# DeltaNet with Fourier mixing: an inversion given to 4 steps a slot instead of 6, its end and load 12's products placed in the mixing, one state copy on ScalarE

## The chip, the cores and the metric

One core of a Trainium2 chip runs the whole kernel in one launch. The metric is the device time of the core in microseconds. The engines are TensorE (PE, with its weight loads as PEld), VectorE (DVE), ScalarE (ACT), GpSimd (POOL) and SyncE (SP), whose queue issues most DMAs.

## The reference

The first half is a delta-rule recurrence over 4 batches x 8 heads, 768 tokens, head width 48; the second half takes its output as 4 x 768 x 384, adds the real part of a 2-D Fourier transform, normalizes, and applies a two-layer network of width 1536. All is float32.

```python
k_n = k / (norm(k) + 1e-6)
for t in range(768):                       # per batch and head, state is 48 x 48
    y[t] = q[t] @ state
    state += beta[t] * outer(k_n[t], v[t] - k_n[t] @ state)
x = y as (batch, token, head*48)
u = x + real(fft(fft(x, axis=token), axis=feature))
un = (u - mean(u)) / sqrt(var(u) + 1e-6)
out = u + relu(un @ w_ch1) @ w_ch2
```

## The kernel before

**Tiling.** The 768 tokens of a batch are cut into 6 loads of 128 (`NL` = 6), so there are 24 loads, `g` = 0 to 23, each of all 8 heads. A load has two chunks of 64 tokens. The recurrence inside a chunk is turned into products with the inverse of a triangular matrix; the state `S` goes from chunk to chunk.

**Inversions.** The triangular matrices of 4 loads (`RL` = 4) are inverted together on VectorE, in round `r`. Rounds 0 to 2 use `invert16`, rounds 3 to 5 `invert` (line 399). The fourth inversion is round 3, for loads 12 to 15. `invert` is a Python generator that yields 77 times: 14 steps of preparation (a transpose at L405, a square root on ScalarE at L412, small operations up to L440), then 31 pairs of a product into `tmp` (L446) and an addition to `M` (L450), and last both transposes (L453 into `A`, L454 into `G`). It has to be complete before `pre_m` of the first load of its round.

**Products of a load.** `pre_m` (line 558) makes for a load the matrices that the recurrence needs: GpSimd writes `MT` (L566) and scales `V` (L569), 16 products of `G` with `GX` go to PSUM (`px`), ScalarE copies them to `XM` (L582, a tile of tag "Q" that has one buffer), 16 more products with `A` (`py`), and ScalarE copies them to `MT` (L593). It yields after `XM` and at its end. Loads before 12 use `pre_m16` instead (Z, ND and MT at L608 to L651).

**The recurrence.** `step(g, c)` for batches after the first has three parts, one to each advance: A, products of `S` with `KT` and their subtraction from `V` on VectorE (L701); B, products of `V` with `MT`, copied to `U` by ScalarE (L711); C, products of `U` with `K`, added to the state `S` by VectorE (L742), or, for the first chunk of a batch, copied (L740). `outputs` makes the rows `x` (L765 on ScalarE, L775 on VectorE).

**Order.** `period(g, side)` runs one load in 6 slots (`SLOTS`). Slots 0 to 2 hold A, B, C of the first chunk and 3 to 5 those of the second; for the first load of a batch slot 0 is empty. In each slot come first these parts and pieces of the next loads' preparation, then some steps of the inversion under way (`advance(inv, n)`), then pieces of the folds, and last `side`, the network's products (`ph`, `po`) of the batch before, which fill TensorE. Round r+1 is begun in slot 1 of the second load of round r (load 9 for the fourth inversion). The order of instructions on each engine is the order of these calls. Loads 6 and 7 are an exception: there only TensorE has its order by hand, and the other engines are ordered by the framework's scheduler.

**Folds and mixing.** After the loads of a batch, `folds` (L798 to L816) adds and subtracts halves of `x` for the transforms; `fourier` is advanced 10 times: 4 parts with the transform over the tokens (`evt`, `odt`), and 6 with the transform over the features (`dtab`), each with a ScalarE copy to the tile `Q` (L876, the same single buffer as `XM`), four VectorE operations on `x` (L885 to L888) and the statistics (L892, L893; `rstd` on GpSimd). Between the parts come 12 pieces of `side`.

The lines that place the inversion and load 12's `pre_m` before the change:

```python
pieces[3 if fresh else 1].append(pm)          # fresh: g is the last load of a round
pieces[5 if fresh else 3].append(pm)
...
if i == (2 if r + 1 < R16 else 3) and fresh and inv:
    drain(inv)
...
elif inv:
    advance(inv, 8 if r + 1 < R16 else 6)
```

Load 11 is both the last load of round 2 and the last of batch 1.

Of the kernel before, what the change touches and what calls it, by code (L numbers as in the profile page):

```python
# [15 lines left out]
ACT = mybir.ActivationFunctionType  # L16
# [4 lines left out]
RL = 4  # L21
RING = 7
V16 = 16
R16 = 3
# [40 lines left out]
def kernel(  # L65
# [10 lines left out]
    nc = tc.nc  # L76
# [3 lines left out]
    NL = S // L  # L80
# [19 lines left out]
    def ps_pair():  # L100
        return ps.tile([128, 2, 512], F32, tag="pair", bufs=2, name="pair")

    def ps_one():
        return ps.tile([128, 512], F32, tag="one", bufs=2, name="one")
# [4 lines left out]
    def mm(o, lhsT, rhs, start, stop=True):  # L109
        nc.tensor.matmul(o, lhsT=lhsT, rhs=rhs, start=start, stop=stop, skip_group_check=True)  # L110
# [570 lines left out]
    def step(g, c):  # L681

        b, n = divmod(g, NL)
        begin = n == 0 and c == 0
        s0 = S.get((b, 2 * n + c))
        if b > 0:

            if c == 0:
                Us[g] = wk.tile([128, 2, 4, D], F32, tag="U0", bufs=2, name="U")
            K, MT, V = pre[g]  # L690
            U0, KT = Us[g], KTs[g]
            R, U = V[:, c], U0[:, c]
            if not begin:
                pw = ps_pair()
                for jj in range(2):
                    for hh in range(2):
                        for jp in range(2):
                            mm(pw[full[hh], jp, D * jj:D * jj + D],
                               KT[lo[jp], hh, jj, c * C:c * C + C], s0[lo[jp], hh, jj, :], jj == 0)
                R4 = R.rearrange("p (jj jp) e -> p jp jj e", jp=2)  # L700
                nc.vector.tensor_tensor(  # L701
                    R4, R4, pw[:, :, 0:2 * D].rearrange("p a (j e) -> p a j e", e=D),
                    op=ALU.subtract)
                yield
            pu = ps_one()
            for j in range(4):
                for hh in range(2):
                    mm(pu[full[hh], D * j:D * j + D],
                       MT[full[hh], 4 * c + j].rearrange("p b t -> p (b t)"), R[full[hh], j, :],
                       j == 0)  # L710
            nc.scalar.activation(U.rearrange("p j e -> p (j e)"), pu[:, 0:4 * D], ACT.Copy)  # L711
            yield
        else:
            K, WT = pre[g]
            U = Us[g][:, c]
        if not begin and b == 0:
            pw = ps_pair()
            for jj in range(2):
                for hh in range(2):
                    for jp in range(2):  # L720
                        mm(pw[full[hh], jp, D * jj:D * jj + D], WT[lo[jp], hh, c, jj, :],
                           s0[lo[jp], hh, jj, :], jj == 0)
            nc.vector.tensor_tensor(
                U.rearrange("p (jj jp) e -> p jp jj e", jp=2),
                U.rearrange("p (jj jp) e -> p jp jj e", jp=2),
                pw[:, :, 0:2 * D].rearrange("p a (j e) -> p a j e", e=D), op=ALU.subtract)
            yield
        if not (n == NL - 1 and c == 1):
            s1 = wk.tile([128, 2, 2, D], F32, tag="S", bufs=4, name="S")
            S[(b, 2 * n + c + 1)] = s1  # L730
            pk = ps_pair()
            for jj in range(2):
                for jp in range(2):
                    for hh in range(2):
                        mm(pk[full[jp], hh, D * jj:D * jj + D], K[full[hh], 4 * c + 2 * jj + jp, :],
                           U[full[hh], 2 * jj + jp, :], jj == 0)
            pk = pk[:, :, 0:2 * D]
            s1v = s1.rearrange("p h j e -> p h (j e)")
            if begin:
                nc.vector.tensor_copy(s1v, pk)  # L740
            else:
                nc.vector.tensor_tensor(s1v, s0.rearrange("p h j e -> p h (j e)"), pk,  # L742
                                        op=ALU.add)
            yield
# [226 lines left out]
    def advance(gen, n=1):  # L971
        for _ in range(n):
            if next(gen, "end") == "end":
                return False
        return True

    def drain(gen):
        for _ in gen:
            pass
# [31 lines left out]
    pm = inv = late = None  # L1011

    def period(g, side):


        nonlocal pm, inv, late, done, fold
        b, n = divmod(g, NL)
        r, li = divmod(g, RL)
        more = g + 1 < NLT
        last_round = (r + 1) * RL >= NLT  # L1020
        load_k(g + 2)
        c0, c1 = step(g, 0), step(g, 1)
        if n > 0:
            pieces = [[c0], [c0], [c0], [c1], [c1], [c1]]
        else:
            pieces = [[], [c0], [c0], [c1], [c1], [c1]]
        behind = [[] for _ in range(SLOTS)]
        if late:

            for i in (1, 2) if n == 1 and b == 1 else (0,):  # L1030
                pieces[i].append(late)
        if n + 1 < NL:
            late = outputs(g)
            if g > NL:
                pieces[4].append(late)
        else:

            pieces[5] = []
        fresh = more and li == RL - 1
        if more:  # L1040
            nq = pre_q(g + 1)
            behind[0].append(nq)
            pieces[2].append(nq)
            if g + 1 >= RL * R16:
                pm = pre_m(g + 1)
                pieces[3 if fresh else 1].append(pm)
                pieces[5 if fresh else 3].append(pm)
            elif g + 1 >= 2 * RL:
                pm = pre_m16(g + 1)
                if not fresh:  # L1050
                    behind[0].append(pm)
                for i in range(4):
                    pieces[i + (2 if fresh else 1)].append(pm)
        if not last_round and r > 1:
            if li == 0:
                load_beta(r + 1)
            keys = {0: ((0, 1), (2, 3), (4, 5)), 1: ((0, 1),)}.get(li, ())
            for i, (s0, s1) in enumerate(keys):
                k4 = pre_a(RL * (r + 1) + 3 * li + i)
                behind[s0].append(k4)  # L1060
                pieces[s1].append(k4)
        for i in range(SLOTS):
            if i == (2 if r + 1 < R16 else 3) and fresh and inv:
                drain(inv)
                inv = None
            for p in pieces[i]:
                advance(p)
            if i == 5 and n + 1 == NL:
                o = outputs(g)
                drain(o)  # L1070
                late = None
            if li == 1 and i == 1 and r > 1 and not last_round:
                inv = invert(r + 1)
            if g == NL:
                advance(inv, 5)
                advance(conv, 2 if i < 5 else 4)
            elif inv:
                advance(inv, 8 if r + 1 < R16 else 6)
            if n + 2 >= NL and 0 < i < 5:

                if n + 2 == NL and i == 1:
                    fold = folds(b)
                advance(fold, 2)
            at = SLOTS * n + i + 1
            if b > 1:
                want = 2 + (PIECES - KEEP - 2) * at // (SLOTS * NL)
            else:

                want = 2 + KF + (2 + 2 * KF) * at // (2 * SLOTS)
                if n > 1:  # L1090
                    want = 4 + 3 * KF + (PIECES - KEEP - 4 - 3 * KF) * (at - 2 * SLOTS) // (
                        SLOTS * (NL - 2))
            for p in behind[i]:
                advance(p)
            advance(side, want - done)
            done = max(want, done)
        load_v(g + 2)
# [3 lines left out]
    with tc.manual_schedule(engines=engines):  # L1101
# [212 lines left out]
        inv = invert16(2)  # L1314
# [5 lines left out]
    with tc.manual_schedule(engines=engines):  # L1320
        for b in range(1, B):
            for g in range(max(NL * b, NL + 2), NL * (b + 1)):
                period(g, side)

            advance(side, KEEP - 12)
            drain(fold)
            f, then = fourier(b), mlp(b)
            done = 0
            for i in range(4 + NC):
                advance(f)  # L1330
                advance(side, 12 * (i + 1) // (4 + NC) - done)
                done = 12 * (i + 1) // (4 + NC)
                if i in (6, 8):
                    advance(then)
            drain(side)
            side, done = then, 2
        drain(side)
# [30 lines left out]
```

## Time and profile before

| | us |
|---|---|
| median of 3 runs (742.43 to 745.95) | 743.56 |
| the profiled execution | 744.35 |
| its span, first to last instruction | 742.6 |
| TensorE busy in it | 689.8 |
| VectorE busy in it | 377.5 |
| ScalarE busy in it | 262.7 |
| GpSimd busy in it | 79.5 |
| mean granted clock of TensorE | 0.975 |

The profiled execution's own time is 0.79 us over the median and 1.75 us over its span. In the profile a row of the timeline has start, length, engine, line, operation, output and inputs, and in brackets the idle time before it and what ended it. L110 is the line of the helper for all matrix products and L113 of that for transposes on TensorE, so these are told apart by their tiles. Times are counted from the span's start: load 9 begins near 234 us, load 10 at 252.8, load 11 at 275.4, the mixing of batch 1 at 302.2, and load 12 at 332.7.

### The profile page before, as it was taken

The page shows a single profiled execution, that of the slowest core. Times are in us where ns is not written, and L with a number is a line of the kernel's source. Part 1 is how long each engine was busy: PE and PEld are TensorE (multiplying, and loading weights), DVE is VectorE, ACT ScalarE, POOL GpSimd, SP SyncE. Part 2 cuts the span into 40 slices and gives each one's busy share as a digit, 9 for nine tenths or more (in the row PEclk, how much of TensorE's full clock was granted, in tenths as well). Part 3 has the DMA queues.
Part 4 walks back from the last instruction along what each step waited for, and adds up shares of the span by engine and source line. Part 5 has one row for each costly group of instructions (what it writes and reads, how often), then busy time and mean ns, then how long its engine had stood idle before and what let it go on. Part 6 is the DMA issues. An engine that isn't in the chain of part 4 may idle for free.

```text
span 742.6 us, 23085 instructions
## 1 busy us (share of the span) xinstructions
PE 689.8 (93%) x10176; PEld 529.9 (71%) x10176; DVE 377.5 (51%) x957; ACT 262.7 (35%) x641; POOL 79.5 (11%) x138
## 2 busy tenths in 40 slices
PE   6877989977999978999999999999999999999998
PEld 4576878756767656878768778777677688777684
DVE  5877887699622996170596228288211241600000
ACT  5544763796324212224323343133223121211120
POOL 8000001120000101021100220030112100200000
PEclk9799989999999997999999999999999999999999
DMA  9842452153123211003212211001110000000000
GB/s 153 221 73 43 118 120 86 24 146 95 25 59 75 46 34 28 1 11 72 40 40 49 45 40 28 11 23 36 42 34 13 12 12 3 20 1 21 11 11 21
DMA packets 108791, 36.10 MB, mean 49 GB/s; under 512 B 101873, under 2 KB 105234, under 8 KB 108690
## 3 DMA queue, kind: packets, MB, share of 16 engines
q1 hardware_dynamic: 106866, 33.86, 21.0%
q8 instruction: 80, 1.31, 0.7%
q0 software_dynamic: 640, 0.43, 0.4%
q10 hardware_dynamic: 1184, 0.33, 0.3%
q14 instruction: 21, 0.17, 0.1%
HBM read 29.88 MB, written 4.72 MB: 47 GB/s over the span
## 4 chain that ended last, share of the span: by engine, by line
PE 73%; DVE 17%; ACT 6%; issue 2%; DMA 1%; DVEq 0%; ACTq 0%
PE po L110 24%; PE ph L110 21%; PE one L110 15%; PE pair L110 9%; PE one L113 2%; DVE M L450 1%; DVE tmp L446 1%; PE ptr L113 1%; PE unread L1114 1%; DVE M L520 1%; DVE tmp L517 1%; ACT GU L395 1%; DMA C<-in_k_dram 1%; DVE w L292 1%; ACT G L385 1%
## 5 line engine op out<-in xcount | busy, mean ns | idle before, releaser
L110 PE MATMUL po<-w,hT 128*128 128x384 f32 x576 | 204.8, 495 | 0.0
L110 PE MATMUL ph<-unT,w 128*128 128x256 f32 x828 | 197.9, 391 | 0.0
L110 PEld LDWEIGHTS ph<-unT,w 128*128 128x128 f32 x828 | 155.6, 193 | 23.3
L110 PEld LDWEIGHTS po<-w,hT 128*128 128x128 f32 x576 | 103.5, 190 | 56.5
L939 ACT ACTIVATE hT<-ph 128x256 f32<-128x256 f32 x138 | 52.9, 383 | 145.9 <-PE ph L110 145.0
L954 DVE TENSOR_TENSOR x<-x,po 128x384 f32<-128x384 f32 x24 | 13.2, 551 | 107.0 <-PE po L110 107.0
L742 DVE TENSOR_TENSOR S<-S,pair 128x192 f32<-128x192 f32 x40 | 14.0, 350 | 71.2 <-PE pair L110 71.1
L110 PEld LDWEIGHTS one<-V,MT 64*64 64x64 f32 x768 | 31.4, 144 | 18.6 <-issue 7.3
L885 DVE TENSOR_TENSOR x<-x,one 128x193 f32<-128x193 f32 x24 | 8.5, 355 | 67.7 <-ACT Q L876 67.7
L110 PE MATMUL one<-V,MT 64*64 64x48 f32 x768 | 36.8, 231 | 3.0 <-DVE V L701 2.7
L450 DVE TENSOR_TENSOR M<-M,tmp 128x31 f32<-128x31 f32 (+15 forms) x93 | 34.5, 371 | 3.2
L446 DVE TENSOR_TENSOR tmp<-A,M 128x31 f32<-128x31 f32 (+15 forms) x93 | 34.1, 367 | 2.5
L701 DVE TENSOR_TENSOR V<-V,pair 128x192 f32<-128x192 f32 x33 | 11.5, 349 | 38.2 <-PE pair L110 28.9
L110 PE MATMUL one<-MT,ND 64*64 64x64 f32 x768 | 29.4, 228 | 1.1 <-ACT MT L649 0.7
L897 POOL TENSOR_SCALAR rstd<-mv 128x1 f32<-128x1 f32 x24 | 6.9, 287 | 218.5 <-DVE mv L893 218.5
L110 PEld LDWEIGHTS one<-dtab,F 97*128 97x128 f32 (+1 forms) x192 | 25.1, 191 | 6.9 <-ACT KT L320 1.8
L320 ACT ACTIVATE QT<-one 128x512 f32<-128x512 f32 x24 | 14.3, 595 | 42.1 <-PE one L113 42.0
L110 PEld LDWEIGHTS one<-MT,ND 64*64 64x64 f32 x768 | 26.9, 143 | 2.5 <-ACT MT L624 1.1
L110 PEld LDWEIGHTS pair<-S,KT 48*64 48x64 f32 x528 | 10.8, 133 | 23.1 <-issue 10.4
L110 PE MATMUL one<-dtab,F 97*128 97x97 f32 (+1 forms) x192 | 26.0, 275 | 1.4 <-ACT KT L320 1.4
L566 POOL TENSOR_TENSOR MT<-A,pack 128x512 f32<-128x512 f32 x12 | 12.8, 1067 | 130.5 <-PE one L110 64.8
L110 PEld LDWEIGHTS pair<-U,K 64*64 64x64 f32 x704 | 15.0, 133 | 15.7 <-issue 12.2
(181 smaller groups left out, 1026.7 us busy)
## 6 DMA issues: line engine op xcount, KB each, us to landing
w<-in_moe_w_ch_dram SPq DMA_DIRECT2D x12, 384.0 KB, 7.4
E<-in_moe_w_ch_dram SPq DMA_DIRECT2D x12, 384.0 KB, 3.0
out_dram<-x SPq DMA_DIRECT2D x24, 192.0 KB, 1.9
K<-in_k_dram SPq DMA_DIRECT2D x92, 48.0 KB, 2.7
V<-in_v_dram SPq DMA_DIRECT2D x92, 48.0 KB, 2.2
C<-in_k_dram SPq DMA_DIRECT2D x18, 192.0 KB, 9.8
Q<-in_q_dram SPq DMA_DIRECT2D x18, 192.0 KB, 3.3
w<-in_q_dram SPq DMA_DIRECT2D x6, 192.0 KB, 7.6
```

The lines of the kernel that those rows point to most:

```text
L110: nc.tensor.matmul(o, lhsT=lhsT, rhs=rhs, start=start, stop=stop, skip_group_check=True)
L113: nc.tensor.matmul(o, lhsT=src, rhs=ident[0:src.shape[0], 0:src.shape[0]], is_transpose=True, start=start, stop=True, skip_group_check=True)
L292: nc.vector.tensor_tensor(pieces[i - lag][1].rearrange("p c f -> p (c f)"), man0, num0.bitcast(F32), op=ALU.mult)
L320: nc.scalar.activation(dst.rearrange("p h j t -> p (h j t)"), pt, ACT.Copy)
L446: nc.vector.tensor_tensor(t, A[:, j + 1:W, j:j + 1].broadcast_to([128, n, j + 1]), M[:, j:j + 1, 0:j + 1].broadcast_to([128, n, j + 1]), o ...
L450: nc.vector.tensor_tensor(M[:, j + 1:W, 0:j + 1], M[:, j + 1:W, 0:j + 1], t, op=ALU.add)
L566: nc.gpsimd.tensor_tensor(MT, MTd[:, m8, None, :].broadcast_to([128, 8, 2, W]), m_blk[:, None, :, None].broadcast_to([128, 8, 2, W]), op=A ...
L701: nc.vector.tensor_tensor(R4, R4, pw[:, :, 0:2 * D].rearrange("p a (j e) -> p a j e", e=D), op=ALU.subtract)
L742: nc.vector.tensor_tensor(s1v, s0.rearrange("p h j e -> p h (j e)"), pk, op=ALU.add)
L885: nc.vector.tensor_tensor(near, near, pb[:, 0, 0:MH + 1], op=ALU.add)
L939: nc.scalar.activation(hT[:, fc, :], ph, ACT.Relu)
L954: nc.vector.tensor_tensor(x[:, T, :], x[:, T, :], po, op=ALU.add)
```

## The change

`lone` is true for load 11 alone. The fourth inversion (`r + 1 == R16`) is advanced by 4 steps in each slot instead of 6. In load 11 it is not drained, and load 12's `pre_m` is not put into slots 3 and 5. In the loop over the mixing's 10 parts the inversion is advanced by 3 steps in each of parts 0 to 2 and drained in part 3; then `pre_m` of load 12 is advanced once in each part until it is over (parts 4 and 5). The condition on `NL * (b + 1) % RL` holds for batch 1 only among those with an inversion under way. Apart from that the first state of batch 1 (load 6, first chunk) is copied out of PSUM by ScalarE instead of VectorE. Loads, weights and all other calls stay.

```diff
-            if begin:
+            if begin and b == 1:
+                nc.scalar.activation(s1v, pk, ACT.Copy)
+            elif begin:
                 nc.vector.tensor_copy(s1v, pk)
...
         fresh = more and li == RL - 1
+
+        lone = fresh and n + 1 == NL
...
                 pm = pre_m(g + 1)
-                pieces[3 if fresh else 1].append(pm)
-                pieces[5 if fresh else 3].append(pm)
+                if not lone:
+                    pieces[3 if fresh else 1].append(pm)
+                    pieces[5 if fresh else 3].append(pm)
...
-            if i == (2 if r + 1 < R16 else 3) and fresh and inv:
+            if i == (2 if r + 1 < R16 else 3) and fresh and inv and not lone:
                 drain(inv)
                 inv = None
...
             elif inv:
-                advance(inv, 8 if r + 1 < R16 else 6)
+                advance(inv, 8 if r + 1 < R16 else 4 if r + 1 == R16 else 6)
...
             for i in range(4 + NC):
                 advance(f)
                 advance(side, 12 * (i + 1) // (4 + NC) - done)
                 done = 12 * (i + 1) // (4 + NC)
+                if inv and NL * (b + 1) % RL == 0:
+                    if i < 3:
+                        advance(inv, 3)
+                    elif i == 3:
+                        drain(inv)
+                    elif not advance(pm):
+                        inv = None
                 if i in (6, 8):
                     advance(then)
```

## The prediction

> **What bounds the kernel now.** I read the engine totals and the chain of waits first. TensorE is busy for 93% of the span and carries 73% of the chain; VectorE carries 17%, though it is busy only half of the time. So most stages run at TensorE's pace, and only the stages in which VectorE is in the chain can give anything.
>
> ```profile
> PE 689.8 (93%) x10176; PEld 529.9 (71%) x10176; DVE 377.5 (51%) x957; ACT 262.7 (35%) x641; POOL 79.5 (11%) x138
> PE 73%; DVE 17%; ACT 6%; issue 2%; DMA 1%; DVEq 0%; ACTq 0%
> ```
>
> The chain in order of time shows where: from 254.4 to 286.0 us it is almost only VectorE, and most of it L446, L450, L453 and L454, which are `invert(3)`. Its last lines (start, length, what):
>
> ```profile
> 278.36 1.00 DVE M L450
> 279.38 0.96 DVE tmp L446
> ...
> 282.20 1.97 DVE A L453
> 284.17 1.83 DVE G L454
> 286.00 0.23 DVE S L742
> ...
> 286.27 0.52 PE pair L110 x16
> ```
>
> From 286.27 to 332 it is TensorE alone. I then asked for the busy time of each engine in the stretch of the inversion and in the one behind it, up to the start of load 12 (two rows), and in slices of 4 us at the inversion's end:
>
> ```profile
> 243.90:287.80 43.90, 35.30 (x687) 25.98 (x686) 41.64 (x102) 8.69 (x20) 6.92 (x7) 0.95 0.18 39
> 287.80:332.70 44.90, 44.32 (x304) 34.69 (x305) 18.23 (x54) 11.88 (x33) 4.18 (x10) 0.94 0.04 9
> ...
> 276.00:280.00 4.00, 4.00 (x39) 2.99 (x33) 3.83 (x9) 0.69 (x2) 1.81 (x2) 0.57 0.26 53
> 284.00:288.00 4.00, 2.04 (x51) 1.57 (x50) 3.97 (x7) 0.55 (x2) 1.83 (x2) 0.81 0.11 22
> 288.00:292.00 4.00, 4.00 (x23) 2.90 (x24) 1.39 (x5) 1.25 (x4) 0.00 (x0) 0.50 0.00 0
> ```
>
> The columns are PE, PEld, DVE, ACT, POOL, the granted clock, DMA share and rate. In the first stretch VectorE is full (41.6 of 43.9) and TensorE idles 8.6; in the second TensorE is full and VectorE is free for 26.7. TensorE's timeline names the waits (in brackets) and shows a second cost, a lower clock behind the two longest of them: six `ph` products take 2.71 us at 277.16 and 2.93 at 287.72, against 1.56 elsewhere.
>
> ```profile
> 267.68 0.60 PE L110 MATMUL one<-V,MT 64*64 64x48 f32 x13 [1.31 <-DVE V L701]
> 275.40 0.45 PE L110 MATMUL pair<-S,KT 48*64 48x48 f32 x16 [2.28 <-DVE S L742]
> 277.16 2.71 PE L110 MATMUL ph<-unT,w 128*128 128x256 f32 x6
> 286.27 0.52 PE L110 MATMUL pair<-S,KT 48*64 48x48 f32 x16 [1.96 <-DVE S L742]
> 287.72 2.93 PE L110 MATMUL ph<-unT,w 128*128 128x256 f32 x6
> ```
>
> For the second edit I looked at load 6:
>
> ```profile
> 175.19 0.35 DVE L740 COPY S<-pair 128x192 f32<-128x192 f32 x1
> 175.60 0.45 PE L110 MATMUL pair<-S,KT 48*64 48x48 f32 x16 [2.91 <-DVE S L740]
> 179.71 0.67 PE L110 MATMUL one<-V,MT 64*64 64x48 f32 x16 [0.88 <-DVE V L701]
> ```
>
> TensorE is free at 172.69, the product is done at 169.4, and the copy waits in VectorE's queue until 175.19.
>
> **What the Trainium skill says.** *Perfetto Trace Analysis*, Tensor Engine Instruction: VectorE, ScalarE and GpSimd work their queues strictly in order. The trace agrees: the copy's input is ready 5.8 us before it runs. *TensorE: Matmul & The Clock Gate*, What's actually happening: the clock is at one half after an idle window of about 3.4 us, which runs freely. Here single waits of 2.28 and 1.96 us, with smaller ones near, are enough (0.57 and 0.50 above), so I go by the trace. *SBUF — State Buffer*, Who interferes with whom: a VectorE instruction with two SBUF inputs is held up by a GpSimd one that reads SBUF. The trace agrees: the L450 and L446 steps beside the folds on POOL take 1.06, 1.06 and 0.90 us at 255.6 to 258.7, against some 0.38.
>
> **Part 1, the inversion spread out.** The generator has 77 steps: 14 of preparation, 62 alternating L446 and L450 (at their largest one each 0.46 us, start to start), and one with both transposes (1.97 each). Before, 6 steps go into each slot from load 9's slot 1, so all are over in load 11's slot 1. After, 4 go into each of 17 slots (68), and 3 into each of the first three parts of the mixing, so the last 9, with both transposes, fall where VectorE has 26.7 us free. No instruction is added; load 12's `pre_m` moves from slots 3 and 5 of load 11 to parts 4 and 5 of the mixing.
>
> Within a slot the recurrence's VectorE operation stands ahead of the slot's steps, and TensorE needs it at the start of the next slot, 0.40 us after it begins (V at 254.43, product at 254.83). So TensorE begins slot i+1 at the later of its own end of slot i and VectorE's end of slot i-1 plus 0.40. I lay out the slots with the timeline's durations (PE work; other VectorE work; four steps; both ends). For load 9 this gives 252.5 (PE, 252.8 before) and 253.4 (VectorE).
>
> ```
> slot   PE work  other  4 steps   PE ends  DVE ends  PE waited
> 10.0   1.5      0.7    3.2       254.0    257.3
> 10.1   3.1      0.0    1.5       257.3    258.8     0.3 (ACT, Z)
> 10.2   3.3      2.5    1.6       260.6    262.9
> 10.3   2.8      1.4    1.7       263.5    266.0
> 10.4   3.5      1.3    1.8       267.0    269.0
> 10.5   1.9      0.3    1.8       268.8    271.1
> 11.0   2.9      0.7    3.1       272.4    274.9     0.6
> 11.1   2.0      0.0    1.8       274.4    276.7
> 11.2   2.4      1.9    1.7       276.7    280.4     0.4
> 11.3   1.8      0.9    1.7       278.9    283.0     0.4
> 11.4   2.0      0.7    1.6       282.8    285.2     1.9
> 11.5   7.7      4.0    1.4       290.5    290.6
> ```
>
> The steps of 10.0 and 11.0 hold 1.9 and 1.3 us lost to the folds on POOL. "Other" is V, S, LQ, Z, MT, the folds and x. In 11.5 VectorE has eight fold operations and TensorE five groups of `ph`. The mixing's first product then starts at 290.7 instead of 302.2. I add 1.6 for one drop of the clock behind the 1.9 us wait (what the first drop cost: 1.15 on `ph` and 0.46 on the transposes at 276.25), so 292.3. The mixing took 302.2 to 332.7 = 30.5. It now also holds load 12's two product groups (0.62 each in load 13's, so 1.3) and a new wait.
>
> **The new wait.** `XM` of `pre_m` shares the one buffer of tag Q with the mixing's `Q`. From the first output product: its VectorE part is done with Q 2.6 us later, TensorE comes to px at 3.5, XM is written to 4.9, the second output product ends at 5.1, py at 7.0. Only then may ScalarE write the second Q (7.05 to 7.4), and VectorE frees its PSUM buffer at 8.1. The third output product, next in TensorE's order, waits 1.1 us. Behind Q on ScalarE stand the two L593 copies, which nobody awaits for 8 us. GpSimd's MT and V (1.04 and 0.83) follow the first rstd and end at 6.3, ahead of the second mv at 9.6: hidden. So load 12 starts at 292.3 + 30.5 + 1.3 + 1.1 = 325.2, 7.5 earlier. The same layout with six steps puts the kernel before at 304.5 (299.9, and 4.6 for its two drops), 2.3 later than it was; taking half of that error as common gives 7.5 + 1.1 = 8.6. No DMA is moved past another by the spreading: the loads stay at their slots, and SP's queue is nearly idle there (DMA share 0.18 and 0.04).
>
> **Part 2, the copy on ScalarE.** One VectorE copy (0.35) becomes one ScalarE copy; the same shape out of PSUM takes 0.33 there (L711). TensorE's 2.91 us wait at 175.60 should go. But VectorE runs without a gap from 171 to 195.8, and the next operation that TensorE needs, V at 179.31, keeps its place in that queue behind the steps of its slot; it gains only the copy's 0.27. The wait moves to the product at 179.71. I take 0.3. The upper end is 1.9: V is placed earlier by the automatic order that loads 6 and 7 have outside TensorE, and the wait comes back at Z, which needs `G` (L523, done at 194.0). The lower end is -0.5: the copy stands in front of the sqrt at 170.83, which VectorE awaits, or that order changes for the worse.
>
> **Sum.** 8.6 + 0.3 = 8.9. The profiled execution took 744.35 (742.6 of it span), 0.8 over the median of 743.56; so 735.4 against the former, 734.7 as a median. Later stages add nothing either way: TensorE waits only some 3.7 us for others from 332 on.
>
> **The rivals.**
> - *Half of it.* VectorE is freed, but TensorE waits on links that the longer queue hid (Z, U, x behind ScalarE), or the folds, which end level with TensorE in 11.5, come late. For it: the margin there is nothing, and VectorE still ends behind TensorE in each slot of loads 10 and 11. Against it: ScalarE is busy 8.7 us of 43.9. Gain 4.5, 739.1.
> - *More.* All waits (8.6) and both drops (4.6) go, and part 2 brings 1.9: 15.1 less 1.1, 729.6. Against it: load 11's slots leave VectorE 2 to 3 us short.
> - *Nothing.* The fewer steps per slot only move the waits, as in part 2, into the mixing. Against it: VectorE has 26.7 us free there. 743.6.
> - *Slower.* The one Q buffer makes the output products serial, and the waits halve the clock in that stage. Three waits of 1.1 (3.3) and half clock for all 14.0 us behind the second product cost 17.3, against 10.0 otherwise gained (8.9 and the 1.1 counted): 750.9. It decides from 6.7 us of work at half clock. Against it: a wait of 1.31 at 267.68 left the clock at full, and each drop ended within some 7 us.
>
> **How the numbers follow.** Chances: forecast 0.60, half 0.17, more 0.12, nothing 0.06, slower 0.05. About 0.5% (3.7 us) is what a measurement of this kernel can tell from no change. "Half" lies at 4.5 and may fall within it (0.02 of its chance): faster 0.87, same 0.08, slower 0.05. The range 730.5 to 741.0 takes part 2's ends, one drop of the clock more or less and most of "half".
>
> **What would show it.** L446 and L450 reach into the mixing; L453 and L454 lie after the last fold; TensorE idles less than 4.5 us between load 9 and the mixing; the third output product waits about 1 us; ScalarE writes S near 170 to 172, and the product with V near 179.4 is late instead. The mixing starting later than 297, or load 12 later than 329, would make the forecast wrong.

## The result, and the profile after

The changed kernel takes 739.02 us in the median of 9 runs (737.99 to 742.37), the kernel before 744.62 in 9 (742.43 to 747.36). The ratio is 0.9932, 95% interval 0.9910 to 0.9953: 5.1 us faster by the ratio, with 3.5 to 6.7 in the interval. The profiled execution took 737.99 us with a span of 736.2.

Between the two profiled executions the difference of 6.4 us has three parts. Load 6 lost: from its first product of `U` with `K` to the first product of `Z` with `GU` it is 29.0 us after and 27.6 before. Load 9 to load 12 gained: load 12 starts at 326.33 instead of 332.73, 6.4 earlier, though the product of Z with GU had come 1.2 later (197.81 against 196.59); so 7.6 were gained in between. (The stretch of load 6 lost 1.4, but it starts 0.1 earlier.) From load 12 to the end both take 409.87 us: nothing is gained or lost later.

Engine totals and chain shares of the page of the changed kernel: VectorE does the same work, but its share of the chain falls from 17% to 12%.

```profile
PE 687.4 (93%) x10176; PEld 527.3 (72%) x10176; DVE 378.0 (51%) x956; ACT 262.4 (36%) x642; POOL 79.7 (11%) x138
PE 78%; DVE 12%; ACT 7%; issue 2%; DVEq 0%; ACTq 0%
```

Busy time in the two stretches that stand for those of before (start and end, length, then PE, PEld, DVE, ACT, POOL, granted clock, DMA share, rate). TensorE idles 2.9 us of 36.5 in the inversion's stretch (8.6 of 43.9 before), and VectorE works 27.5 us in the mixing's instead of 18.2.

```profile
245.00:281.50 36.50, 33.65 (x660) 24.78 (x660) 32.42 (x81) 9.06 (x21) 5.07 (x5) 1.00 0.22 46
281.50:326.30 44.80, 42.88 (x330) 33.38 (x331) 27.48 (x75) 11.35 (x32) 5.96 (x12) 0.96 0.04 10
```

VectorE's timeline after: the last fold of batch 1, then the rest of the inversion with both transposes, then a pause until the first output product of the mixing. (L450 and L453 have kept their lines; the folds are two lines lower.)

```profile
291.62 0.36 DVE L818 TENSOR_TENSOR O<-O 128x190 f32<-128x190 f32 x1
...
294.04 1.98 DVE L453 STREAM_TRANSPOSE A<-M 128x1024 f32<-128x1024 f32 x1
295.88 2.00 DVE L454 STREAM_TRANSPOSE G<-M 128x1024 f32<-128x1024 f32 x1
307.39 0.36 DVE L887 TENSOR_TENSOR x<-x,one 128x193 f32<-128x193 f32 x1 [9.51 <-ACT Q L878]
```

TensorE's timeline after, in load 11 and in the mixing. The waits of 2.28 and 1.96 for `S` are now 0.18 and 0.26. The 1.61 stands at a product with `V` that had no wait before; the `ph` products behind it run at a lower clock for a time (2.27 for six instead of 1.56). The mixing begins at 292.98. Its third output product (314.35) has the wait that the change adds: it is the one behind `A,XM`.

```profile
270.66 0.45 PE L110 MATMUL pair<-S,KT 48*64 48x48 f32 x16 [0.18 <-DVE S L744]
278.16 0.45 PE L110 MATMUL pair<-S,KT 48*64 48x48 f32 x16 [0.26 <-DVE S L744]
281.70 0.67 PE L110 MATMUL one<-V,MT 64*64 64x48 f32 x16 [1.61 <-DVE V L701]
282.30 2.27 PE L110 MATMUL ph<-unT,w 128*128 128x256 f32 x6
292.98 1.14 PE L110 MATMUL one<-evt,E 128*97 128x193 f32 x6
...
312.53 0.69 PE L110 MATMUL one<-A,XM 32*32 32x32 f32 x32
314.35 1.13 PE L110 MATMUL one<-dtab,F 97*128 97x97 f32 x8 [1.13 <-ACT MT L593]
```

Load 6 after, from the timeline of all engines and then from TensorE's: the copy now runs as soon as its input is there, but `V` stands at 179.00, almost where it stood before (179.31), TensorE waits 3.69 us for it in one piece, and the twelve `ph` products behind take 4.54 us instead of 2.86.

```profile
169.38 0.33 ACT L740 ACTIVATE S<-pair 128x192 f32<-128x192 f32 x1
...
179.00 0.36 DVE L701 TENSOR_TENSOR V<-V,pair 128x192 f32<-128x192 f32 x1
```

```profile
179.42 0.67 PE L110 MATMUL one<-V,MT 64*64 64x48 f32 x16 [3.69 <-DVE V L701]
180.01 4.54 PE L110 MATMUL ph<-unT,w 128*128 128x256 f32 x12
```

So the open questions were three: whether the copy is a loss and by what; what of the gain comes from the spread and what from the move; and what the new wait and the waits left over cost.

### The profile page after: what moved, and what is told of

It is laid out like the page before. It is cut to its first block, busy times and chain, and to the rows that moved or that the text cites. A ratio compares the mean times of both kernels' runs of the same rounds, so it can differ in the third digit from the quotient of the medians.

```text
span 736.2 us, 23086 instructions
## 1 busy us (share of the span) xinstructions
PE 687.4 (93%) x10176; PEld 527.3 (72%) x10176; DVE 378.0 (51%) x956; ACT 262.4 (36%) x642; POOL 79.7 (11%) x138
## 4 chain that ended last, share of the span: by engine, by line
PE 78%; DVE 12%; ACT 7%; issue 2%; DVEq 0%; ACTq 0%
PE po L110 25%; PE ph L110 22%; PE one L110 16%; PE pair L110 10%; PE one L113 2%; PE unread L1119 2%; PE ptr L113 1%; DVE tmp L446 1%; DVE M L450 1%; ACT GU L395 1%; ACT G L385 1%; PE pf L110 1%; DVE MT L651 1%; DVE A L405 1%; ACT wtmp L277 0%
## 5 line engine op out<-in xcount | busy, mean ns | idle before, releaser
L450 DVE TENSOR_TENSOR M<-M,tmp 128x31 f32<-128x31 f32 (+15 forms) x93 | 35.3, 379 | 3.2
L711 ACT ACTIVATE U<-one 128x192 f32<-128x192 f32 x36 | 11.9, 330 | 38.8 <-PE one L110 38.8
```

What stands on the lines that cost most here:

```text
L450: nc.vector.tensor_tensor(M[:, j + 1:W, 0:j + 1], M[:, j + 1:W, 0:j + 1], t, op=ALU.add)
```

## The experiments

All ratios are to the kernel before, measured beside it on the same chip, with 95% intervals.

| kernel | median us (before) | ratio | interval |
|---|---|---|---|
| the change | 739.02 (744.62) | 0.9932 | 0.9910 to 0.9953 |
| part1_only | 735.28 (743.96) | 0.9902 | 0.9871 to 0.9933 |
| part2_only | 746.20 (743.96) | 1.0031 | 1.0010 to 1.0052 |
| spin_in_wait | 737.74 (743.96) | 0.9924 | 0.9901 to 0.9947 |
| xm_own_buffer | 738.85 (743.96) | 0.9933 | 0.9910 to 0.9957 |
| move_only | 745.95 (744.64) | 1.0022 | 1.0005 to 1.0038 |
| spread_drained | 749.12 (744.64) | 1.0056 | 1.0039 to 1.0072 |
| three_steps | 735.22 (744.64) | 0.9863 | 0.9828 to 0.9899 |
| load6_order | 737.71 (744.64) | 0.9909 | 0.9875 to 0.9944 |
| spin_five | 737.31 (745.52) | 0.9892 | 0.9868 to 0.9917 |
| three_steps_xm | 732.12 (745.52) | 0.9829 | 0.9797 to 0.9862 |
| three_steps_xm_spin | 733.33 (745.52) | 0.9856 | 0.9819 to 0.9893 |

Single runs of one kernel lie 3 to 11 us apart, so steps of 1 us are read from the profiles, by the length of a stretch, and not from the medians. U,K stands for load 6's products of `U` with `K`, and Z,GU for the first product of `Z` with `GU` behind them.

**part1_only and part2_only: the two edits apart**

```diff
 part1_only, against the change
-            if begin and b == 1:
-                nc.scalar.activation(s1v, pk, ACT.Copy)
-            elif begin:
+            if begin:
 part2_only, against the kernel before: the same lines the other way round
```

> The inversion spread as in the change, the first state of batch 1 copied by VectorE as before. Theory: the copy's edit costs 1.2 us (its wait, 3.7 us in one piece, halves TensorE's clock), so without it the kernel is 7.5 us faster than before, about 737.0, and 1.2 to 1.5 faster than the whole change; the product with V of load 6 waits 0.9, not 3.7, and the twelve products behind it take 2.9 us, not 4.5. Rival (the copy gives its 0.3 and the low clock is chance): same as the whole change or 0.3 slower.

> Only the first state of batch 1 is copied by ScalarE; the inversion is as before. Theory: the wait of 2.9 us goes, the product with V waits 3.7 in its place, the clock drops for the twelve products behind (4.5 us instead of 2.9), so load 6 ends 1.2 later and the kernel is 1.2 us slower than before. Rival (position in the queue only, no clock): 0.3 faster. Rival (V moves up): up to 1.9 faster.

In part1_only's timeline of TensorE both waits of load 6 are as before, and the clock stays up. Load 11's wait of 1.61 us is there as well, this time with no lower clock behind it (1.56).

```profile
175.75 0.45 PE L110 MATMUL pair<-S,KT 48*64 48x48 f32 x16 [2.91 <-DVE S L740]
179.87 0.67 PE L110 MATMUL one<-V,MT 64*64 64x48 f32 x16 [0.88 <-DVE V L701]
180.46 2.86 PE L110 MATMUL ph<-unT,w 128*128 128x256 f32 x12
...
280.84 0.67 PE L110 MATMUL one<-V,MT 64*64 64x48 f32 x16 [1.61 <-DVE V L701]
281.44 1.56 PE L110 MATMUL ph<-unT,w 128*128 128x256 f32 x6
```

In part2_only's, load 6 is as in the change:

```profile
179.07 0.67 PE L110 MATMUL one<-V,MT 64*64 64x48 f32 x16 [3.70 <-DVE V L701]
179.67 4.54 PE L110 MATMUL ph<-unT,w 128*128 128x256 f32 x12
```

The copy by itself makes the kernel slower, by 0.7 to 3.9 us of the interval; both rivals, 0.3 and 1.9 faster, fall. The inversion's edit by itself has a ratio of 0.9902 (7.3 us), against the 7.6 of the profiled executions. Its interval overlaps with the change's, so that part1_only is the faster of the two rests on the profiles (27.7 us from U,K to Z,GU, against 29.0). part2_only's profile has the same 29.0, but its whole execution is only 0.15 us longer than that of before (744.50 against 744.35): it starts load 6 half a microsecond earlier and has other drops of the clock behind it.

**spin_in_wait and spin_five: is it the clock?**

```diff
         for i in range(SLOTS):
+            if g == NL and i == 4:
+                spin(8)          # spin_five: spin(5)
```

`spin(n)` puts `n` products of 128x384 on TensorE whose result nothing reads; the edit is against the change.

> The whole change, with eight unused 128x384 products put on TensorE in load 6 ahead of the product with V, where it waits 3.7 us. No result depends on them. Theory (the clock is what the copy's edit costs): they take about 2.6 us of the wait, the twelve ph products behind run at full clock (2.9 instead of 4.5 us), and the kernel is 1.4 to 1.7 us faster than the whole change. Rival (TensorE is only late, the clock comes from elsewhere): no gain or up to 1 us slower.

Eight took twice the time expected, so they outlasted the wait: `V` was written from 177.52, and its product came at 179.52. From VectorE's and TensorE's timelines:

```profile
177.52 0.34 DVE L701 TENSOR_TENSOR V<-V,pair 128x192 f32<-128x192 f32 x1
```

```profile
174.16 5.43 PE L1121 MATMUL unread<-evt 128*128 128x384 f32 x16
179.52 0.67 PE L110 MATMUL one<-V,MT 64*64 64x48 f32 x16
180.12 2.86 PE L110 MATMUL ph<-unT,w 128*128 128x256 f32 x12
```

The clock stayed up, but most of its gain went into the delay: from the first U,K to the second takes 15.57 us, against 15.65 in the change and 14.12 before. With five:

> The whole change with five unused 128x384 products in load 6's wait instead of the eight of spin_in_wait, which took 5.4 us instead of the 2.6 expected (0.67 each, not 0.33) and held the product with V back by 1.6. Theory (the clock is what the wait costs): five take 3.4 us and end with the wait of 3.7, the clock stays up, and the profile has the product with V within 0.4 us of V and 2.9 us for the twelve ph products: 1.7 us faster than the whole change in load 6. Rival (the drop comes all the same): 4.5 us for the twelve.

```profile
177.37 3.49 PE L1121 MATMUL unread<-evt 128*128 128x384 f32 x10
181.12 0.67 PE L110 MATMUL one<-V,MT 64*64 64x48 f32 x16 [0.26 <-DVE V L701]
181.71 2.86 PE L110 MATMUL ph<-unT,w 128*128 128x256 f32 x12
```

The same stretch is 13.96 us, 1.69 less than in the change, the whole of the low clock and no more; it is then 0.16 shorter than with the copy on VectorE. So the copy's edit gives something like the 0.27 that its place in the queue was counted to give, and loses it and more to the clock.

**load6_order: is it the place in the queue?**

```diff
 against the change
-                advance(inv, 5)
+                advance(inv, (5, 5, 0, 6, 7, 7)[i])
```

> The whole change (copy on ScalarE), with the steps of the third inversion in load 6 given as 5, 5, 0, 6, 7, 7 by slot instead of 5 each. Theory (V keeps its place behind the steps of slot 2): V comes about 1.5 us earlier, TensorE's wait of 3.7 us falls to some 2.2, the clock stays up, and later waits grow, since VectorE's queue of load 6 and 7 ends no earlier: Z of load 8 bounds the gain; 1.2 to 3 us faster than the whole change. Rival (the scheduler puts V by readiness and not behind those steps): no change in the wait.

From VectorE's and TensorE's timelines:

```profile
178.16 0.35 DVE L701 TENSOR_TENSOR V<-V,pair 128x192 f32<-128x192 f32 x1
178.42 0.35 DVE L502 RECIPROCAL n<-n 128x32 f32<-128x32 f32 x1
```

```profile
178.56 0.67 PE L110 MATMUL one<-V,MT 64*64 64x48 f32 x16 [2.38 <-DVE V L701]
179.16 4.54 PE L110 MATMUL ph<-unT,w 128*128 128x256 f32 x12
...
197.95 0.69 PE L110 MATMUL pair<-QT,KT 48*64 48x64 f32 x32 [1.55 <-DVE S L744]
```

`V` now stands ahead of the reciprocal that opens the moved steps, and the wait fell from 3.69 to 2.38: the place in the queue is shown. The clock dropped all the same, which I had not expected at 2.4 us. The stretch from U,K to U,K became 1.3 us shorter (14.34), but the queue's end came back as a wait for `S` (1.55), so that up to Z,GU it is 29.2, against 29.0 in the change. Behind that wait the clock drops once more (4.54 us for eight `po` products at 199.51, 2.85 in the change). The bound holds, at nothing; the ratio of 0.9909 overlaps with the change's and doesn't show the 1.2 to 3 us expected.

**move_only and spread_drained: the move or the spread?**

```diff
 move_only, against part1_only
-                advance(inv, 8 if r + 1 < R16 else 4 if r + 1 == R16 else 6)
+                advance(inv, 8 if r + 1 < R16 else 6)
 spread_drained, against the kernel before
-                advance(inv, 8 if r + 1 < R16 else 6)
+                advance(inv, 8 if r + 1 < R16 else 4 if r + 1 == R16 else 6)
```

> Six steps of the fourth inversion a slot as before, so that all of it ends in load 11, but load 12's pre_m in the mixing as in the change; the state copy on VectorE. Theory (the gain is VectorE work taken out of loads 9 to 11): none of it stays, TensorE waits some 8 us for VectorE in loads 10 and 11 as before, and the mixing has the 1.1 us wait for Q: about 1 us slower than before. Rival (the gain comes from load 12's products leaving load 11): 5 us or more faster than before.

> Four steps a slot as in the change, but what is left is drained at slot 3 of load 11, ahead of load 12's pre_m there as before; the state copy on VectorE. Theory (VectorE's queue up to load 11's second chunk sets the end): 21 steps of some 11 us stand in one piece ahead of V of slot 3, TensorE waits there about 9 us and loses its clock; the mixing starts at 303 to 306 and the kernel is 1 to 4 us slower than before. Rival (it is the even spread that gains): 5 us or more faster than before.

Either half alone loses: 1.6 us and 4.2 us by the ratios. In move_only TensorE's waits in loads 9 to 11 are those of before, and the mixing has its new one. That it loses rests on the ratio: from Z,GU to load 12 its profiled execution is 1.6 us shorter than that of before, for the drop behind the wait of 1.96, which cost 3.0 there, did not come in it. In spread_drained there is one wait in place of many, in TensorE's timeline:

```profile
282.21 0.45 PE L110 MATMUL pair<-S,KT 48*64 48x48 f32 x16 [0.24 <-DVE S L742]
...
295.83 1.06 PE L110 MATMUL one<-G,GX 32*32 32x32 f32 x32 [13.18 <-DVE G L454]
296.83 2.93 PE L110 MATMUL ph<-unT,w 128*128 128x256 f32 x6
```

It stands at load 12's products, which come ahead of V's in slot 3, and not at V, as I had put it; it is 13.2 us and not 9. What gains is VectorE work taken out from in front of what TensorE needs in loads 9 to 11, and that takes both: few enough steps a slot, and no user of `G` and `A` before the mixing. move_only's profile shows one more thing: a low clock behind the old wait of 2.91 us in load 6.

```profile
179.04 0.68 PE L110 MATMUL pair<-S,KT 48*64 48x48 f32 x16 [2.91 <-DVE S L740]
179.65 5.49 PE L110 MATMUL ph<-unT,w 128*128 128x256 f32 x12
```

With the copy on VectorE and this wait left in, it is there in two profiled executions (move_only, spread_drained; 16.1 and 16.0 us from U,K to U,K) and not in four (14.1).

The traces show what decides. In the clock records of all 13 profiled executions the clock changes only on a grid of 3.413 us, whose position differs from one execution to the next. Here are windows of that grid (start and end, length, then PE, PEld, DVE, ACT, POOL, granted clock, DMA share, rate): the two that share the wait of 2.91 before, then the one that holds it in move_only and the one behind that, then the one in the change that has most of the 3.69.

```profile
170.46:173.88 3.42, 2.23 (x11) 1.62 (x9) 2.95 (x12) 2.80 (x7) 0.00 (x0) 1.00 0.30 64
173.88:177.29 3.41, 1.69 (x22) 1.51 (x23) 3.41 (x14) 1.58 (x3) 0.00 (x0) 1.00 0.57 189
...
175.03:178.44 3.41, 1.10 (x6) 0.62 (x4) 3.41 (x14) 2.86 (x7) 0.00 (x0) 1.00 0.46 129
178.44:181.85 3.41, 2.81 (x21) 2.36 (x22) 3.41 (x12) 1.10 (x2) 0.00 (x0) 0.50 0.40 115
...
177.19:180.61 3.42, 1.19 (x19) 1.09 (x20) 3.42 (x14) 1.71 (x4) 0.00 (x0) 1.00 0.02 4
```

Before, an edge of the grid cuts the wait in two, and TensorE is busy for 2.23 and 1.69 us of the two windows. In move_only one window has the whole wait, TensorE is busy for only 1.10 us of it, and the next window has half the clock; so it is in the change, where 1.19 us are left. The 13 traces have 2618 windows at full clock. TensorE was busy for less than 49% of 53 of them, and half clock followed each; it was busy for more than 68% of 2455, and half clock followed none; of the 110 between, it followed 32. From this an estimate: a wait of 2.91 can be cut so that no window falls under 57% (1 less 1.455 of 3.413), but one of 3.69 leaves a window at 46% or less wherever the edge falls. So part 2 turned a drop that comes in some executions into one that comes in all. Its price on average is then lower than in the first pair of profiles: from U,K to Z,GU the six executions with the copy on VectorE and the wait left in take 28.2 us in the mean, and the three with the copy on ScalarE and nothing else in load 6 changed take 29.0. These are few; the ratio of part2_only has the price at 0.7 to 3.9 us.

**xm_own_buffer: the new wait**

```diff
 against the change
-        XM = wk.tile([128, 8, W], F32, tag="Q", name="XM")
+        own = g == RL * R16
+        XM = wk.tile([128, 8, W], F32, tag="tmp" if own else "Q", bufs=2 if own else None, name="XM")
```

> The whole change, with XM of load 12 in a buffer of the inversion's tmp, free by then, instead of the one buffer of the mixing's Q. Theory: the third output product of the mixing no longer waits 1.1 us; ScalarE writes the second Q about 2 us earlier; 1.1 us faster than the whole change. Rival (the wait is handed on to the PSUM buffers, which px and py take from the same two): the wait stays at 0.5 to 1.1 and the gain is under 0.5.

From ScalarE's timeline: `Q` follows `XM` at once, where in the change it waited for the products of `A` with `XM` (313.33).

```profile
309.36 0.76 ACT L583 ACTIVATE XM<-one 32x256 f32<-32x256 f32 x2 [2.91 <-PE one L110]
310.46 0.33 ACT L879 ACTIVATE Q<-one 128x193 f32<-128x193 f32 x1 [0.34 <-ACT XM L583]
```

The mixing is 32.16 us long (292.07 to 324.23) instead of 33.35: the wait was 1.1 us and did not come back at the PSUM buffers. In the ratio this doesn't show. The bracket at 314.35 in the change names `MT` of L593, but here the third output product starts at 312.25 and that copy only at 312.42. So that copy is not what it waits for. These products take two PSUM buffers in turn, and the third needs the second's, which VectorE reads until 314.32 in the change, late because `Q` was late. A wait of this size can also cost a drop: in spin_in_wait the clock falls behind it (2.26 us for four `po` products instead of 1.48), and the mixing takes 34.63 us.

**three_steps and three_steps_xm: the waits left over**

```diff
 against part1_only; three_steps_xm has the lines of xm_own_buffer too
-                advance(inv, 8 if r + 1 < R16 else 4 if r + 1 == R16 else 6)
+                advance(inv, 8 if r + 1 < R16 else 3 if r + 1 == R16 else 6)
...
-                        advance(inv, 3)
+                        advance(inv, 9)
```

> As part1_only (copy on VectorE), with three steps a slot and nine in each of the first three parts of the mixing. Theory: the waits left between load 9 and the mixing for S and V (0.2, 0.3 and 1.6 us) and the drop of the clock that can follow the last go, the waits on ScalarE's Z (0.9) and on XM (1.1) stay; VectorE has 11 us of inversion in the mixing and is done 4 us before its first output product: 2.0 us faster than part1_only, up to 3.6 where that one has the drop. Rival (the end then moves to the folds or to G, needed by load 12's first products): no gain.

In three_steps, load 11's products with `S` and `V` come with no wait, and the inversion ends 2.4 us ahead of VectorE's first operation on an output product, closer than expected. TensorE's and VectorE's timelines:

```profile
276.58 0.45 PE L110 MATMUL pair<-S,KT 48*64 48x48 f32 x16
...
278.53 0.67 PE L110 MATMUL one<-V,MT 64*64 64x48 f32 x16
279.13 1.56 PE L110 MATMUL ph<-unT,w 128*128 128x256 f32 x6
```

```profile
298.24 2.01 DVE L454 STREAM_TRANSPOSE G<-M 128x1024 f32<-128x1024 f32 x1
302.69 0.36 DVE L885 TENSOR_TENSOR x<-x,one 128x193 f32<-128x193 f32 x1 [2.44 <-ACT Q L876]
```

From Z,GU to the mixing it is 91.75 us, against 93.78 in part1_only: 2.0, as expected; the ratios' intervals overlap. With both cures:

> three_steps (copy on VectorE, three steps a slot) with XM of load 12 in the free buffer of tmp, as in xm_own_buffer: the fastest version that the runs so far point to. Theory: the 1.1 us wait of the third output product goes too, nothing else moves: 1.1 us faster than three_steps, 9.5 to 10.5 faster than before. Rival (something else ends last in the mixing, such as G or ScalarE's copies): as three_steps.

The mixing takes 32.16 us there too; the profiled execution took 731.96. This is the fastest version by the median: 732.12, ratio 0.9829, 10.3 to 15.1 us by the interval below the kernel before. Its interval lies wholly below the change's and overlaps with that of three_steps.

> three_steps_xm with four unused 128x384 products ahead of the product with S of load 6 (2.9 us of wait there; 2.7 us of work). Theory (with the copy on VectorE the drop behind the 2.9 us wait comes in some executions and not in others, 2.5 us or more when it comes): never a drop in load 6, so 0 to 2 us faster in the median than three_steps_xm, and the runs lie closer together. Rival (that drop has another cause or is too rare): same as three_steps_xm.

Four spins ahead of the product with `S` of load 6 filled the 2.9 us, and the clock stayed up (2.86 for the twelve `ph`), but three_steps_xm's profile has no drop there either, and the ratio 0.9856 is no better. Single runs from 732.05 to 740.12 lie further apart, not closer. Its profiled execution, the slowest of them, reaches load 6 some 7.7 us later than that of three_steps_xm: ahead of load 6 its trace has five more windows at half clock, 17 us, and the mean granted clock up to there is 0.86 against 0.91. So what sets these two apart lies ahead of load 6, and the drops of the clock there are long enough to account for it (half of 17 us is 8.5).

## Why the prediction was right, and where not

- **What bounds the kernel:** right. VectorE's queue in loads 9 to 11 held TensorE up; move_only and spread_drained show that it needs both the spread and the move.
- **The slots of loads 10 and 11:** right. Predicted waits of TensorE 0.3 (for Z), 0.6, 0.4, 0.4 and 1.9; measured 0.88 for Z, then 0.18, none, 0.26 and 1.61: 2.9 instead of 3.6. (The first 0.4, in row 11.2, is in the table's last column but not in its times, which hold 3.2.) The last stands where it was put, with one drop of the clock behind it that cost 1.5 us (from that product to the mixing 11.28 us, in part1_only, which has the wait and not the drop, 9.75); it was costed at 1.6. The drop is in four of six profiled executions that have the 1.61 us wait, so it was a likely term and not a sure one; that it came in this execution is luck. Of the three slowed steps named beside the folds, the last (0.90) runs beside GpSimd's scaling of `V`; nothing rests on that.
- **The new wait at the one buffer of Q:** right in place, size and chain (VectorE frees the PSUM buffer 8.4 us behind the first output product, 8.1 by the forecast), 1.13 for 1.1, and xm_own_buffer shows its cause. GpSimd's `MT` and `V` were hidden, as said.
- **The mixing:** 33.35 us for 32.9. The first start was put at 292.3 before part 2 and came at 292.98, with 1.2 of that from load 6. The signs named beforehand all came, but that `S` was written at 169.38, ahead of the 170 to 172.
- **The half of the layout's error, 1.1 us, added to the gain:** wrong. The layout without it says 7.5; the profiles say 7.6.
- **Part 2:** this is the step that failed. That TensorE's wait would move to the product with `V`, and that `V` would gain only the copy's 0.27, was right (179.04 by the forecast, 179.00 measured). I took the sum of that, 0.3 faster, as its price, and put the lower end at 0.5 slower. But I let two waits of 2.91 and 0.88 become one of 3.69 without asking what that does to the clock, though I had costed this for load 11. It cost 1.68 us (4.54 for 2.86), and the edit lost 1.2 us in the profile. The Trainium skill (*TensorE: Matmul & The Clock Gate*, What's actually happening) gives an idle window of about 3.4 us; the prediction quoted it and did not hold it against the 3.69 us that it forecast itself. The spins show that it is the idle time, since the drop is gone with TensorE busy.
- **The sum:** 8.9 forecast, 6.4 in the profiles and 5.1 by the ratio; the 2.5 between the first two are 1.1 (the half error) and 1.5 (part 2), less 0.1. That 739.02 lies in the range is owed in part to its width, which took in most of "half": that rival comes nearest in size (4.5), but not by its reason. Of the links that it named only Z showed as a wait, 0.6 us longer than forecast, and TensorE waited less in loads 10 and 11 than forecast. No other rival came true.

## What to carry to other kernels

Where an engine's queue is full in one stage and idle in the next, count per slot what stands in that queue ahead of what the bounding engine needs next; moving such work helps only if its users move with it. A moved step takes its buffers along: look for every one-buffer tag that it shares with its new neighbours. And when a wait is taken away but the next one comes from the same queue, the idle time runs together; cost the longer pause by what it does to TensorE's clock, not only by its length. For that, ask how much of one window of the clock's grid the pause can fill when the grid falls badly, and whether it does so wherever the grid falls.

## What was not expected of the hardware

- The clock drops at shorter pauses than I had thought, and not always at the same pause: behind a wait of 1.13 us in one of seven profiled executions, behind 1.61 in four of six, behind 2.38 in the only one, behind 2.91 in two of six, behind 3.7 in all three. In load 6 the twelve products behind took 1.7 to 2.6 us longer for it. What decides is for how much of a window of 3.413 us TensorE is busy, and so where the grid cuts the pause. The Trainium skill (*TensorE: Matmul & The Clock Gate*, What's actually happening) states a window of 3413 ns that runs freely, and the traces agree; it speaks of an idle window, and here windows in which TensorE was busy for up to 67% were enough. What decides between 49% and 68% isn't shown.
- A 128x384 float32 product takes 0.67 us here, in two halves of 0.34 that the profile lists apart (16 rows for 8 products, 5.43 us).
